# One-layer steps make their memory values behind their opening products, and sixteen output products move behind the second scores

## The chip, the cores and the metric

The kernel runs on one core of one Trainium2 chip. The metric is device time in microseconds (us) of one execution. Three runs of the kernel before gave 1603.28, 1603.80 and 1605.38; the median, 1603.8, is the time before.

## The reference

Four layers run over a sequence of 2048 tokens of width 512: a memory-augmented attention (A), a dense layer (B), and both again with the same weights, each with a layer norm ahead and a residual around it. A goes through the sequence in 64 segments of 32 tokens. Eight memory rows travel from segment to segment, so segment s cannot begin its attention before segment s-1 has given its memory:

```python
for s in range(n_seg):
    h = concat([mem, xs], axis=1)          # 8 memory rows + 32 tokens = 40
    q, k, v = h @ Wq, h @ Wk, h @ Wv       # 32 heads of 128
    scores = (q @ k.T) * scale             # masked; memory rows are seen by all
    p = softmax(where(mask, scores, -1e9))
    o = (p @ v) @ Wo                       # 40 x 512
    mem = o[:8]
    outs.append(o[8:])
```

B is `relu(h @ w1) @ w2` with 1376 hidden units.

## The kernel before

The first and the second attention layer run together, the second four segments behind the first (DELTA = 4). `step(k)` does segment k of layer 0 and segment k-4 of layer 1. So steps 4 to 63 have two layers; steps 1 to 3 have layer 0 alone, steps 64 to 67 layer 1 alone. These are the one-layer steps (`single`). Step 0 stands by itself in `first_step`.

A step runs like this on TensorE (PE):

1. `qk(0)` (L546, L532): the opening query and key products of heads 0 to 15, in three batches of 6, 6 and 4 heads, each batch first queries, then keys: six tiles `qp`. ScalarE (ACT) casts queries to `QT` (L538), VectorE (DVE) casts keys to `KT` (L540). They read `HT`, which holds 8 memory columns and 32 token columns per layer.
2. `block(k, 0, part)`: a first part of the output products of the step before (`output_x`, tile `wox`, L365, L388 or L393: attention rows of the tokens times Wo), used as filling, with pieces of value products (L306) in some steps.
3. `scores` (L566, tile `sp`), then the softmax of heads 0 to 15: maximum, subtraction, sum and reciprocal on DVE, exponential on ACT, the product `P_sb` on GpSimd (POOL).
4. `qk(1)` for heads 16 to 31, a second part of `block`, the second scores and softmax.
5. The dense layer's first product (`dense_h`, L468), the rest of `block`, the dense layer's second product (`dense_y`, L491).
6. `transpose_p` (L608), `weighted_v` (tiles `pv`, L634; reads `Vs`), `output_mem` (tile `wo`, L574: memory rows times Wo).
7. `new_memory` (L764): `wo` is cast to `wm` (L766), small products (tile `mt`, L772) turn it, and two casts copy it: to `HTm` for the values (L783) and to `HT` for queries and keys (L786). In a one-layer step the cast to `HTm` goes first; the timeline shows that the one to `HT` waits for it where the two are on different engines (step 65: "0.76 <-ACT HTm L783").
8. `memory_values(k + 1)` (L708): 32 products `vm` of 512 columns (L717) give the values of the next step's memory rows. ACT casts them (`VmS`, L721), SyncE's queue (SP) stores them to `vmd` in DRAM (L722), and `load_memory_values` (L724) reads them into `Vs` (L727) in the next step.
9. `prepare(k + 1)`: residual adds, statistics of the layer norm (L264, L219, L221), the power on POOL (L222) and the mask for the scores (L558). In a one-layer step the normalized rows `XN` (L227) are written behind the first cast of keys, by `behind` (L858, L550). `transpose_step` (L284) issues their transpose on SP (L289); `turn_p` (L614) issues that of `P_sb` (L615).

What sets the order: PE, DVE, SP and POOL run in a schedule written by hand, so their instructions stand as the program issues them, with `high_priority` only marking parts; ACT's order is chosen by the scheduler. Each engine runs its instructions in order, and a wait holds all that stands behind it on that engine.

The accumulators in PSUM that matter here are the three buffers of the pool `ps_c` (L60, tag "c"). The six tiles `qp` of `qk`, the two `vm`, `mt`, `tp`, some `pv` and, in one-layer steps, `wo` take turns in them; a tile waits until the one before it in its buffer has been read.

In step 67 (LAST) the three products of `keep_busy` (L841, tile `idle`) stand between the last part of `block` and the transposes; their result is used by nobody.

Of the kernel before, what the change touches and what calls it, by code (L numbers as in the profile page):

```python
# [22 lines left out]
def kernel(  # L23
# [260 lines left out]
    def transpose_step(k):  # L284
        if not norm_parts(k):
            return
        t = xnT_tiles[k] = wk.tile([128, NC4, 128], BF, tag="xnT", bufs=1, name="xnT")
        if k <= LAST:
            nc.sync.dma_start_transpose(out=t[:], in_=XN[:])  # L289
        else:  # L290
            tp = transpose_pe(XN)
            nc.scalar.copy(out=t[:], in_=tp[:])
# [81 lines left out]
    def output_x(k, lo, hi):  # L374
        if not 0 <= k <= LAST or ox_span(k) is None:
            return
        r0, r1 = [x % 64 for x in (ox_span(k)[0], ox_span(k)[1] - 1)]
        r1 += 1
        if lo == 0:
            pool, tag = (ps_wo, "wo") if k < LAST else (ps_c, "c")  # L380
            wo_tiles[k] = pool.tile([128, Dm], F32, tag=tag, name="wox")
        for h in range(lo, hi):
            if r1 - r0 == 64:
                halves(wo_tiles[k], OTx[:, h, r0:r1], Wo_sb[:, h, :], h == 0, h == H - 1)
            elif by_heads(k):
                for j in range(2):
                    q = 32 * (2 * (h % 2) + j)
                    nc.tensor.matmul(wo_tiles[k][q:q + 32, 0:256], lhsT=OTx[:, h, r0:r1],  # L388
                                     rhs=Wo_sb[:, h, 256 * j:256 * j + 256], start=(h < 2), stop=(h >= H - 2),
                                     tile_position=(0, q))  # L390
            else:
                for j in range(4):
                    nc.tensor.matmul(wo_tiles[k][32 * j:32 * j + 32, 0:128], lhsT=OTx[:, h, r0:r1],  # L393
                                     rhs=Wo_sb[:, h, 128 * j:128 * j + 128], start=(h == 0), stop=(h == H - 1),
                                     tile_position=(0, 32 * j))
# [290 lines left out]
    def load_values(k, act):  # L686
        for a in act:
            if a == 1 or k == 1:
                nc.sync.dma_start(out=Vs[64 * a + M:64 * a + L, :].rearrange("t (n e) -> t n e", n=NCH),
                            in_=(vd1.pop(k) if a else vd0[0])[:].rearrange("i j t e -> t (i j) e"))  # L690
            elif k >= 4 and k % 4 < 2:
                for u in range(2):
                    lo = M + 2 * M * u
                    nc.sync.dma_start(out=Vs[lo:lo + 2 * M, :].rearrange("t (n e) -> t n e", n=NCH),
                                in_=vmds[k - k % 4 - 4 + 2 * (k % 4) + u][:, :, 2 * M:32, :].rearrange("i j t e -> t (i j) e"))
            else:
                r = SEG * (k % 2)
                nc.sync.dma_start(out=Vs[M:L, :].rearrange("t (n e) -> t n e", n=NCH),
                            in_=vd0[k // 2][:, :, r:r + SEG, :].rearrange("i j t e -> t (i j) e"))
# [30 lines left out]


    def block(k, lo, hi):
        output_x(k - 1, lo, hi)
        groups = values_at(k)
        if split(k):

            rest = [(i, 0, NC4) for i in range(1, len(groups))]
            if k == 1:
                todo = [] if lo == 0 else [(0, 0, 2)] if hi == 16 else [(0, 2, NC4)] + rest
            else:  # L740
                todo = [(0, 0, 2)] if lo == 0 else [(0, 2, NC4)] if hi == 16 else rest
        else:
            todo = [(i, c4, c4 + 2) for i in range(len(groups)) for c4 in range(0, NC4, 2)
                    if lo < 8 * i + 2 * c4 + 2 <= hi]
        for i, c_lo, c_hi in todo:
            p, n = groups[i]
            values0(p, n, c_lo, c_hi, ps_wo if i in (0, 3 if len(groups) == 4 else 2) else None)
# [93 lines left out]
    def keep_busy(n):  # L841

        idle = ps_fill.tile([128, Dm], F32, tag="fill", name="idle")
        for i in range(n):
            nc.tensor.matmul(idle[:], lhsT=ident[:], rhs=Wo_sb[:, i, :], start=True, stop=True)

    def step(k):
        act = layers(k)
        single = len(act) == 1
        cont = [a for a in act if k - DELTA * a + 1 < NSEG]  # L850
        n_x = k // 4 + 3
        has_x = n_x < NXT
        by_pe = k in (1, LAST)
        ahead = has1(k + 1) or not cont
        if k % 4 == 0 and has_x:
            load_xb(n_x)
        with tc.high_priority(offset=PRIO):
            behind = norm_rows.pop(k, None)  # L858
            if k == 1:
                def behind():  # L860
                    normalize(nc.vector, xbs[n_x], xbs[n_x], moments_x(n_x), 0, 128)
            qks = qk(0, act, behind=behind)
            load_values(k, act)
            if k == 1:
                memory_values(k)
                inputs_T(n_x, True)
        part = 4 if k == LAST else 8 if single else 5
        mid = 8 if k == LAST else 16

        light = split(k)  # L870
        block(k, 0, part)
        with tc.high_priority(offset=PRIO):
            transpose_step(k)
            load_memory_values(k, act)
            scores(qks, act)
            softmax(0, act, by_pe)
            if not by_pe:
                turn_p()
        if k % 4 == 3 and has_x:
            inputs_T(n_x)  # L880
        if has0(k + 1):
            load_x(k + 1)
        if k == 1:
            load_dense()
        with tc.high_priority(offset=PRIO):
            qks = qk(1, act)
        if single:
            block(k, part, mid)
        elif light:
            dense_h(k - 2, slice(0, 1))  # L890
            block(k, part, 16)
        else:
            dense_h(k - 2)
        with tc.high_priority(offset=PRIO):
            scores(qks, act)
            softmax(1, act, by_pe)
        if single:
            dense_h(k - 2, slice(0, 1) if k == LAST else slice(None))
            block(k, mid, H)
            if k == LAST:  # L900
                keep_busy(3)
        elif light:
            dense_h(k - 2, slice(1, None))
            block(k, 16, H)
        else:
            block(k, part, H)
        f_mid = 9 if ahead or k == 2 else 5
        if k < LAST:
            dense_y(k - 2, 0, f_mid)
        if not single:  # L910
            add_output(k - 1)
        if k % 4 == 1 and k > 1 and has_x:
            mom["x"] = moments_x(n_x)
        with tc.high_priority(offset=PRIO):
            transpose_p(1)
        if ahead and k < LAST:
            dense_y(k - 2, f_mid, NFC)
        tokens_in(k + 1)
        if k < LAST and spare_T(k + 1) is not None:
            nc.gpsimd.tensor_copy(out=HTm[:, :, 2 * M:32], in_=spare_T(k + 1))  # L920
        with tc.high_priority(offset=PRIO):
            pvs = weighted_v(act)
            outputs(k, pvs)
        if single and k < LAST and ahead:
            add_dense(k - 2)
            store(k - 2)
        if single:
            add_output(k - 1, 0)
        if cont:
            with tc.high_priority(offset=PRIO):  # L930
                pool, tag = (ps_c, "c") if single else (ps_wo, "wo")
                wo = pool.tile([128, Dm], F32, tag=tag, name="wo")
                output_mem(k, wo)
        if not ahead:
            dense_y(k - 2, f_mid, NFC)
        if not single and k < LAST and ahead:
            add_dense(k - 2)
            store(k - 2)
        if cont:
            with tc.high_priority(offset=PRIO):  # L940
                new_memory(k, cont, wo)
        if single:
            add_output(k - 1, 1)
        if not ahead:
            add_dense(k - 2)
            store(k - 2)
        values1(k + 1, 1)
        if cont:
            output_ride(k)
            with tc.high_priority(offset=PRIO):  # L950
                memory_values(k + 1)
        with tc.high_priority(offset=PRIO):
            prepare(k + 1)
        if k % 4 == 2 and k > 2 and has_x:
            normalize(nc.vector, xbs[n_x], xbs[n_x], mom["x"], 0, 128)
# [83 lines left out]
```

## Time and profile before

| what | us |
|---|---|
| median of three runs | 1603.8 |
| profiled execution | 1602.88 |
| its span | 1601.2 |
| PE busy (matmul) | 1569.6 |
| PE busy (weight loads) | 1322.3 |
| DVE busy | 1263.5 |
| ACT busy | 738.6 |
| POOL busy | 347.6 |
| steps 2 and 3 | 69.3 to 108.7 |
| steps 64 to 67 with the end | 1510.9 to 1601.2 |

The granted clock of PE is 1.00 throughout. PE's matmuls overlap, so their busy time says little on how dense the work is; the starts of weight loads (PEld) show gaps better. "Idle before" at a row is the time its engine stood still ahead of it, and the name behind the arrow is what ended it; "issue" is time for which the profile shows nothing that the engine waited for.

### The profile page before, as it was taken

The page shows a single profiled execution, that of the slowest core. Times are in us where ns is not written, and L with a number is a line of the kernel's source. Part 1 is how long each engine was busy: PE and PEld are TensorE (multiplying, and loading weights), DVE is VectorE, ACT ScalarE, POOL GpSimd, SP SyncE. Part 2 cuts the span into 40 slices and gives each one's busy share as a digit, 9 for nine tenths or more (in the row PEclk, how much of TensorE's full clock was granted, in tenths as well). Part 3 has the DMA queues.
Part 4 walks back from the last instruction along what each step waited for, and adds up shares of the span by engine and source line. Part 5 has one row for each costly group of instructions (what it writes and reads, how often), then busy time and mean ns, then how long its engine had stood idle before and what let it go on. Part 6 is the DMA issues. An engine that isn't in the chain of part 4 may idle for free.

```text
span 1601.2 us, 94768 instructions
## 1 busy us (share of the span) xinstructions
PE 1569.6 (98%) x42725; PEld 1322.3 (83%) x42727; DVE 1263.5 (79%) x3112; ACT 738.6 (46%) x1800; POOL 347.6 (22%) x666
## 2 busy tenths in 40 slices
PE   6899999999999999999999999999999999999998
PEld 4677888888888888889888888888888898888876
DVE  4578888888888888888888888878888888787765
ACT  3434444444544444454444445445444544545432
POOL 2012222222222222222222222222222222221210
PEclk9999999999999999999999999999999999999999
DMA  9733343343434334334333433443343334334232
GB/s 370 234 78 74 75 89 88 66 95 86 80 75 88 86 67 97 85 78 78 87 89 63 97 86 78 79 89 87 67 101 82 80 75 82 89 62 101 69 68 39
DMA packets 222532, 146.38 MB, mean 91 GB/s; under 512 B 123976, under 2 KB 216496, under 8 KB 222128
## 3 DMA queue, kind: packets, MB, share of 16 engines
q1 hardware_dynamic: 218976, 136.09, 37.3%
q8 instruction: 335, 5.49, 1.6%
q0 software_dynamic: 3072, 4.20, 1.1%
q14 instruction: 69, 0.57, 0.1%
q10 hardware_dynamic: 80, 0.03, 0.0%
HBM read 65.41 MB, written 45.35 MB: 69 GB/s over the span
## 4 chain that ended last, share of the span: by engine, by line
PE 94%; SPq 2%; DVE 1%; issue 1%; DMA 1%; ACT 0%; POOLq 0%; ACTq 0%; DVEq 0%
PE qp L532 38%; PE wox L365 10%; PE wo L574 8%; PE vm L717 7%; PE v L346 7%; PE hp L468 6%; PE sp L491 5%; PE pv L634 4%; PE sp L566 4%; PE vp L306 3%; PE tp L608 1%; SPq L148 1%; PE xp L439 1%; SPq L134 1%; PE wox L388 1%
## 5 line engine op out<-in xcount | busy, mean ns | idle before, releaser
L538 ACT CAST QT<-qp 128x480 bf16<-128x480 f32 (+3 forms) x408 | 201.5, 494 | 392.9 <-PE qp L532 392.7
L532 PE MATMUL qp<-HT,Wq_sb 128*128 128x80 bf16 (+1 forms) x8704 | 370.2, 200 | 2.6 <-POOL HT L706 1.2
L532 PE MATMUL qp<-HT,Wk_sb 128*128 128x80 bf16 (+1 forms) x8704 | 369.3, 199 | 2.1 <-issue 1.3
L532 PEld LDWEIGHTS <-Wq_sb 128*128 128x128 bf16 x8704 | 326.4, 99 | 34.6 <-issue 27.1
L532 PEld LDWEIGHTS <-Wk_sb 128*128 128x128 bf16 x8704 | 328.5, 100 | 3.1 <-issue 2.7
L540 DVE CAST KT<-qp 128x480 bf16<-128x480 f32 (+3 forms) x408 | 225.1, 565 | 102.6 <-PE qp L532 100.5
L598 POOL TENSOR_TENSOR P_sb<-es,sm 128x320 bf16<-128x320 f32 x185 | 130.8, 721 | 752.5 <-ACT es L588 509.7
L365 PE MATMUL wox<-Wo_sb,OTx 128*64 128x256 bf16 x2880 | 173.6, 273 | 0.0
L582 DVE TENSOR_REDUCE mx<-sp 128x8 f32<-128x320 f32 x256 | 115.1, 487 | 73.5 <-PE sp L566 72.5
L593 DVE TENSOR_REDUCE sm<-es 128x8 f32<-128x320 f32 x256 | 118.9, 465 | 44.3 <-ACT es L588 33.5
L365 PEld LDWEIGHTS <-OTx 128*64 128x64 bf16 x2880 | 150.2, 110 | 2.9
L588 ACT ACTIVATE es<-es 128x320 f32<-128x320 f32 x256 | 110.5, 468 | 58.5 <-DVE es L586 57.9
L717 PE MATMUL vm<-Wv_sb,HTm 128*32 128x512 bf16 x2176 | 136.2, 380 | 0.6 <-DVE HT L786 0.6
L346 PE MATMUL v<-Wv_sb,xnT 128*32 128x512 bf16 x2048 | 129.7, 378 | 0.1
L574 PE MATMUL wo<-Wo_sb,OTm 128*32 128x512 bf16 x2144 | 129.1, 380 | 0.2
L558 DVE CAST sp<-maskb 128x320 f32<-128x320 bf16 x256 | 118.4, 484 | 0.0
L586 DVE TENSOR_TENSOR es<-sp,mx 128x320 f32<-128x320 f32 x256 | 113.8, 483 | 1.5
L717 PEld LDWEIGHTS <-HTm 128*32 128x32 bf16 x2176 | 89.3, 96 | 28.7 <-issue 11.9
L491 PE MATMUL sp<-w_sb,hT 128*64 128x256 bf16 (+4 forms) x1474 | 105.9, 276 | 0.6 <-ACT hT L474 0.5
L468 PE MATMUL hp<-xnT,w_sb 128*128 128x64 bf16 (+3 forms) x2948 | 102.5, 193 | 1.2 <-issue 0.5
L721 ACT CAST VmS<-vm 128x512 bf16<-128x512 f32 x134 | 78.6, 586 | 53.7 <-PE vm L717 53.7
L468 PEld LDWEIGHTS <-w_sb 128*128 128x128 bf16 (+1 forms) x2948 | 95.2, 101 | 2.4 <-issue 1.8
(115 smaller groups left out, 2028.8 us busy)
## 6 DMA issues: line engine op xcount, KB each, us to landing
Vs<-vd SPq DMA_DIRECT2D x96, 256.0 KB
vd<-vst SPq DMA_DIRECT2D x181, 128.0 KB
vmd<-VmS SPq DMA_DIRECT2D x134, 128.0 KB
Vs<-vmd SPq DMA_DIRECT2D x254, 32.0 KB
Vs<-vmd SPq DMA_DIRECT2D x60, 128.0 KB
Wq_sb<-in_A_Wq_dram SPq DMA_DIRECT2D x2, 2048.0 KB
Wk_sb<-in_A_Wk_dram SPq DMA_DIRECT2D x2, 2048.0 KB
Wv_sb<-in_A_Wv_dram SPq DMA_DIRECT2D x2, 2048.0 KB
```

The costliest lines, as they stand in the source:

```text
L346: nc.tensor.matmul(vp[32 * j:32 * j + 32, :], lhsT=tokens[:, c4, :], rhs=Wv_sb[:, c4, n * 512:(n + 1) * 512], start=(c4 == 0), stop=(c4 == ...
L365: nc.tensor.matmul(out[64 * j:64 * j + nr, 0:256], lhsT=lhsT, rhs=rhs[:, 256 * j:256 * j + 256], start=start, stop=stop, tile_position=(0, ...
L468: nc.tensor.matmul(hp[0:fs, fc - f0, 0:n], lhsT=w1_sb[:, c4, fc * 128:fc * 128 + fs], rhs=cols(c4), start=(c4 == 0), stop=(c4 == NC4 - 1))
L491: nc.tensor.matmul(sp_banks[bank][64 * j:64 * j + n, 0:w], lhsT=hT_tiles[d][0:fs, fc, 0:n], rhs=w2_flat[0:fs, fc * Dm + 256 * j:fc * Dm + ...
L532: nc.tensor.matmul(qp[:, hi, 0:ncol], lhsT=W_sb[:, c4, h * Dh:(h + 1) * Dh], rhs=HT[:, c4, a_lo:a_hi, :], start=(c4 == 0), stop=(c4 == NC4 ...
L538: nc.scalar.copy(out=dst[:, 0:nh, a_lo * L:a_hi * L], in_=qp[:, 0:nh, 0:ncol])
L540: nc.vector.tensor_copy(out=dst[:, 0:nh, a_lo * L:a_hi * L], in_=qp[:, 0:nh, 0:ncol])
L558: nc.vector.tensor_copy(out=sp_tiles[a], in_=maskb2)
L574: nc.tensor.matmul(wo[32 * j:32 * j + 32, :], lhsT=OTm[:, h, n, 2 * M * c:2 * M * c + 4 * M], rhs=Wo_sb[:, h, :], start=(h < 4), stop=(h > ...
L593: nc.vector.tensor_reduce(out=sm[:], in_=es[:], axis=AX.X, op=ALU.add)
L598: eng.tensor_tensor(out=P, in0=es[:], in1=sm[:].unsqueeze(2).to_broadcast([128, 8, L]), op=ALU.mult)
L717: nc.tensor.matmul(vp[32 * j:32 * j + 32, :], lhsT=HTm[:, c4, :], rhs=Wv_sb[:, c4, n * 512:(n + 1) * 512], start=(c4 == 0), stop=(c4 == NC ...
```

## The change

Three things. `memory_values(k + 1)` at the end of a step is kept only where the next step has two layers; a one-layer step makes its own memory values behind `qk(0)` and `load_values`, and there also issues its `transpose_step` (step 1 made its own already). The one-layer step's `block` is cut anew: `part` goes from 8 to 0 (from 4 to 0 in the last step), `mid` from 16 to 8 (from 8 to 4). So heads 0 to 7 go where heads 8 to 15 stood, behind `qk(1)`, and heads 8 to 15 go behind the second scores. The conditions in `block` for step 1 are rewritten so that its value products stay where they were. And `keep_busy` in the last step makes two idle products instead of three.

```diff
     def block(k, lo, hi):
+        if lo == hi:
+            return
         output_x(k - 1, lo, hi)
...
             if k == 1:
-                todo = [] if lo == 0 else [(0, 0, 2)] if hi == 16 else [(0, 2, NC4)] + rest
+                todo = [(0, 0, 2)] if lo == 0 else [(0, 2, NC4)] + rest
...
             qks = qk(0, act, behind=behind)
             load_values(k, act)
+            if single:
+                transpose_step(k)
+                memory_values(k)
             if k == 1:
-                memory_values(k)
                 inputs_T(n_x, True)
-        part = 4 if k == LAST else 8 if single else 5
-        mid = 8 if k == LAST else 16
+
+        part = 0 if single else 5
+        mid = 4 if k == LAST else 8
...
         with tc.high_priority(offset=PRIO):
-            transpose_step(k)
+            if not single:
+                transpose_step(k)
             load_memory_values(k, act)
...
             if k == LAST:
-                keep_busy(3)
+                keep_busy(2)
...
             output_ride(k)
-            with tc.high_priority(offset=PRIO):
-                memory_values(k + 1)
+            if len(layers(k + 1)) == 2:
+                with tc.high_priority(offset=PRIO):
+                    memory_values(k + 1)
```

So six steps change their order: 2, 3 and 64 to 67.

## The prediction

> **What bounds the kernel now.** I read the page first, then the waits of PE, then the timeline of the six one-layer steps that change: steps 2 and 3 (69 to 109 us) and steps 64 to 67 (1511 to 1601 us). From the page:
>
> ```profile
> PE 94%; SPq 2%; DVE 1%; issue 1%; DMA 1%; ACT 0%; POOLq 0%; ACTq 0%; DVEq 0%
> L717 PE MATMUL vm<-Wv_sb,HTm 128*32 128x512 bf16 x2176 | 136.2, 380 | 0.6 <-DVE HT L786 0.6
> q8 instruction: 335, 5.49, 1.6%
> ```
>
> The chain that ended last is PE for 94% of the span, and the change neither adds nor removes a matmul except one idle one (a pair of instructions fewer among 42,727 weight loads). So time can come only from gaps of PE in these six steps. They are small, and of two kinds.
>
> The first kind is a wait for a cast. This is the start of step 3 in the timeline (columns: start, length, engine, line, operation, count, idle time before and its releaser):
>
> ```profile
> 89.34 0.18 DVE L786 CAST HT<-mt 128x32 bf16<-128x32 f32 x1
> 89.54 1.45 PEld L717 LDWEIGHTS <-HTm 128*32 128x32 bf16 x32 [0.48 <-issue]
> 91.41 0.67 PEld L532 LDWEIGHTS <-Wq_sb 128*128 128x128 bf16 x24 [0.42 <-DVE R L371]
> ...
> 93.00 0.48 DVE L558 CAST sp<-maskb 128x320 f32<-128x320 bf16 x1
> 93.51 0.41 DVE L540 CAST KT<-qp 128x240 bf16<-128x240 f32 x1
> 93.95 1.09 DVE L227 TENSOR_SCALAR XN<-R,mv,rstd 32x512 bf16<-32x512 f32 x2
> ...
> 94.97 0.62 DVE L540 CAST KT<-qp 128x240 bf16<-128x240 f32 x2
> 95.41 0.35 PEld L566 LDWEIGHTS <-QT 128*40 128x40 bf16 x16 [0.21 <-issue]
> ```
>
> From 89.34 to 93.51 DVE is busy without a pause (residual adds, statistics, mask), and only then casts the first keys. PE hides this now: it makes the memory values (89.54 to 91.41, 1.87 us with the 0.42 in which they drain) ahead of the query and key products.
>
> The second kind is a pause that no semaphore explains ("issue"). In step 2, weight loads alone:
>
> ```profile
> 80.02 0.32 PEld L532 LDWEIGHTS <-Wk_sb 128*128 128x128 bf16 x10 [0.97 <-issue]
> 80.38 0.34 PEld L388 LDWEIGHTS <-OTx 128*32 128x32 bf16 x16
> 80.93 0.27 PEld L566 LDWEIGHTS <-QT 128*40 128x40 bf16 x16 [0.21 <-issue]
> 81.24 1.25 PEld L468 LDWEIGHTS <-w_sb 128*128 128x128 bf16 x44
> 82.52 0.78 PEld L388 LDWEIGHTS <-OTx 128*32 128x32 bf16 x32
> 83.29 0.57 PEld L491 LDWEIGHTS <-hT 128*32 128x32 bf16 x10
> 84.30 0.42 PEld L491 LDWEIGHTS <-hT 128*32 128x32 bf16 x8 [0.44 <-issue]
> ```
>
> From pause to pause are 10+16+16+44+32+10 = 128 pairs of weight load and matmul, 256 instructions. Queue q8 moved 335 packets and 5.49 MB, 16 KB each, and 85,452 PE instructions over 335 is 255. So PE's own instructions come in blocks of 256, and a block lasts at least as long as the next one takes to arrive: from pause to pause 4.28 (80.02 to 84.30), 4.27 (75.75 to 80.02), 3.75 and 3.89 (1578.26, 1582.01, 1585.90). I take 3.9, with 3.7 and 4.3 as ends. The 40-column products run at 0.025 us a pair, 3.3 us a block: too fast. [...]
>
> **The change, part by part.** The built program's order shows that it does what it says: 32 vm products go from ahead of the opening products to behind them, 16 output products (8 heads) from ahead of the first scores to behind the second, in steps 2, 3 and 64 to 67; step 1 and the two-layer steps keep their order, and so does DVE. Prices: opening products 3.3 us (step 65, 1533.46 to 1536.77); vm 1.85 (1531.61 to 1533.46); eight heads 0.55 in the old place (0.34 of loads and 0.21 of drain), 0.39 in the new one (half of the 32 at 82.52); with 64 rows (step 64) 0.8 in both.
>
> New waits. The opening products now wait for HT, cast after HTm: in steps 65 to 67 HT's cast ends 0.2 later and its signal takes 0.1, so +0.29. Then three PSUM banks serve six batches and two vm tiles, and by the built program's waits these stand behind key casts that DVE, whose order is unchanged, cannot start sooner: the first at the end of the mask, the second 1.44 us after it (1554.63 and 1556.07 in step 66; behind the two XN rows).
>
> Step 3, in full: HT ends at 89.52, products from 89.62, a batch of 24 each 0.60, so the fifth ends loading at 92.42. The sixth reuses its bank and waits for its cast: 93.05 to 93.45. vm's first tile takes the bank of the first keys: 93.92 plus 0.11 = 94.03 (in step 65 KT's cast ends at 1537.20 and the scores load at 1537.32). Its second takes that of the second keys: cast from 94.95 to 95.36, so 95.47 where the products would be there at 94.98, +0.5. Scores at 94.03 + 1.85 + 0.5 = 96.4, against 95.41: **+1.0**. Behind them the eight heads cost 0.39, of which the wait for P_sb ahead of the transposes (0.41) hides all. Counted on from 84.30, a block begins 18 pairs into vm (95.6), so the next arrives at 99.5 (needed 99.4) and the one after at 103.4 (needed 103.0): +0.5. Step 3: **+1.5**. Queued behind these waits on PE is everything up to the new memory; no other engine fills in.
>
> Step 2: DVE is free at 71.43, but the block that paused PE at 72.02 is now needed at 70.8, 54 pairs into the opening products, and I take it to come no sooner. Scores end at 76.2 (75.98 now); the pauses at 80.02 and 84.30 recur at about 80.4 (0.65) and 84.2 (0.3): **+0.15**. Step 64: start +0.3, sixth batch at 1514.07 behind the key cast, scores at 1516.4 (1517.05 now), pause 0.3 instead of 0.26, heads +0.8: **+0.15**. Step 65: +0.29, fifth batch +0.27, vm +0.6 (1536.0), scores +0.53; the pause of 0.68 at 1539.77 goes, since vm's slow instructions now stand inside that block, heads +0.39, a pause of 0.3 for one of 0.13 in the dense products: **+0.4**. Step 66: +0.29, sixth batch +0.8 (key cast 1554.63), scores +0.5; the pause of 0.41 becomes 0.55, heads +0.39: **+0.95**. Step 67: +0.28 and +0.48, scores +0.4. From here PE is paced by blocks: now 1578.26, 1582.01, 1585.90; after, the first is crossed unpaused at 1578.6, then 1582.5 and 1586.4: **+0.5**. The removed idle matmul (0.1) lies in that wait and is worth nothing.
>
> Covers. SP's queue: the transposes of XN now go ahead of the vmd stores, and turn_p behind both. In step 3 the second store issues at about 97.4, its loads some 2.5 later (I bound a landing by the 2.3 us of the R load on the page), turn_p at about 100.3, against 99.13 now; PT and Vs are needed at 105: 2 us spare. If that were gone, it would cost its excess directly on PE.
>
> Sum: 0.15 + 1.5 + 0.15 + 0.4 + 0.95 + 0.5 = **+3.65 us** on the profiled execution (span 1601.2 in a run of 1602.88, so 1.7 around it): 1606.5. The median shown, 1603.8, stands 0.9 above that run: **1607.4**.
>
> **The rivals.** A, not slower: the pauses do not come back, because vm (1.85 us for 32 pairs) now splits the run of fast products and gives the blocks time. It decides from a block arriving below 3.3 us after the last. Then step 2 gives -0.9 (the transposes follow P_sb 3.8 behind scores at 80.1), 3 +1.05, 64 -0.15, 65 +0.1, 66 +0.4, and 67 -1.3 (pv released by P_sb at about 1584.6, not by a block at 1585.90): -0.8, a median of 1603.0. For it: steps where vm, v and wo run show no pause. Against it: no interval between pauses is below 3.7. [...]
>
> B, slower still: blocks take 4.3, as in step 2, everywhere. Seven blocks of mine are limited (two in step 3, one each in 64, 65 and 66, two in 67), 0.4 each: +2.8, a median of 1610.2. For it: more DMA now meets these blocks (stores and loads beside turn_p). Against it: the last steps show 3.75 and 3.89.
>
> That the change does not happen is excluded by the built order.
>
> **How the numbers follow.** Forecast 0.6, A 0.2, B 0.2. The forecast's own spread, from blocks of 3.7 to 4.3 and cast waits 0.2 either way a step, is +2 to +5; about 0.2%, 3.2 us, is what a measurement of this kernel can tell from no change, and the forecast lies above it in 0.38 and below it in 0.22. B is all slower; A is within 0.2% but for 0.04. So slower 0.58, same 0.38, faster 0.04. The range takes in A at its lower end and B with a little: 1602.5 to 1610.8.
>
> **What would show it.** Right: in steps 3, 65 and 66 PE idle ahead of vm or of a batch of qp, released by KT (L540), and pauses by "issue" of 0.3 to 0.7 at every 128th pair; the scores of step 3 start 7.06 us after HT's cast begins, now 6.07. Wrong: no wait for KT (then the banks serve otherwise than I read), no pauses (A), or pv waiting for Vs or PT (a cover gone). If the opening cast waits fall under 0.3 a step, the change gains.

## The result, and the profile after

The changed kernel takes 1605.1 us (median of 22 runs, 1603.4 to 1609.8), the kernel before, run beside it, 1602.1 (22 runs, 1599.5 to 1605.4). The ratio is 1.0023, 95% interval 1.0016 to 1.0029: 3.7 us slower (2.6 to 4.6). The two medians alone differ by 3.0; the text goes by the ratio. The forecast was +3.65 us. Its 1607.4 stands higher mostly because it was counted from a median of three runs, 1603.8. The prediction had called 0.2% the line between slower and the same: the measured 0.23% (0.16 to 0.29) is clear of no change, but not of that line.

The page of the changed kernel, span 1603.4:

```profile
PE 89%; DVE 2%; issue 0%; ACT 0%; DMA 0%; POOLq 0%; ACTq 0%; DVEq 0%
L717 PE MATMUL vm<-Wv_sb,HTm 128*32 128x512 bf16 x2176 | 136.4, 380 | 1.3 <-DVE KT L540 1.2
q8 instruction: 335, 5.49, 1.5%
```

PE is still most of the chain that ended last (89%, before 94%). Ahead of the memory values (vm) PE now stands idle for 1.3 us instead of 0.6, and what ends it is no longer the cast of HT but the cast of keys. The instruction blocks on q8 are as many as before (335).

Step 3 in the timeline of the changed kernel:

```profile
89.05 0.18 DVE L788 CAST HT<-mt 128x32 bf16<-128x32 f32 x1
89.35 0.68 PEld L532 LDWEIGHTS <-Wq_sb 128*128 128x128 bf16 x24 [0.58 <-PE mt L774]
...
92.71 0.48 DVE L558 CAST sp<-maskb 128x320 f32<-128x320 bf16 x1
...
92.83 0.45 PEld L532 LDWEIGHTS <-Wk_sb 128*128 128x128 bf16 x15 [0.52 <-issue]
93.22 0.41 DVE L540 CAST KT<-qp 128x240 bf16<-128x240 f32 x1
...
93.69 1.05 PE L717 MATMUL vm<-Wv_sb,HTm 128*32 128x512 bf16 x16 [0.31 <-DVE KT L540]
93.69 0.74 PEld L717 LDWEIGHTS <-HTm 128*32 128x32 bf16 x16 [0.29 <-issue]
...
94.68 0.62 DVE L540 CAST KT<-qp 128x240 bf16<-128x240 f32 x2
...
95.12 1.05 PE L717 MATMUL vm<-Wv_sb,HTm 128*32 128x512 bf16 x16 [0.39 <-DVE KT L540]
95.12 0.55 PEld L717 LDWEIGHTS <-HTm 128*32 128x32 bf16 x15 [0.69 <-issue]
...
96.09 0.27 PEld L566 LDWEIGHTS <-QT 128*40 128x40 bf16 x16 [0.42 <-issue]
```

DVE is as busy as before up to its mask (92.71) and casts the first keys behind it; all 3112 of its instructions start in that trace in the order in which the program issues them. But PE has no memory values left to do in the meantime. Its sixth batch stands 0.52, the first vm tile 0.29 and the second 0.69 (weight loads), each until a buffer of `ps_c` has been read (the sixth batch until that of the fifth has, since the two others still hold keys that DVE has not cast). The scores load 7.04 us after the cast of HT begins (96.09 less 89.05); it was 6.07.

What PE waited for in the last four steps (1511 to 1602 us; total, times, longest), first the kernel before, then the changed one:

```profile
PE qp L532 <- issue: 1.4, 4, 0.6
PE pv L634 <- issue: 0.6, 1, 0.6
PE hp L468 <- issue: 0.5, 1, 0.5
```

```profile
PE qp L532 <- DVE KT L540: 1.2, 3, 0.5
PE pv L634 <- issue: 0.5, 1, 0.5
PE vm L717 <- DVE KT L540: 0.5, 1, 0.5
```

Here the wait for keys came (1.7 us; 0.3 of it, at 1583.1, stands ahead of the second key products of step 67 and is no part of the opening), and most of the pauses by issue went (2.5 to 0.5). That is why the two executions differ by little in these steps. The lengths of the steps, from the weight load of one step's mt to that of the next, in us:

| kernel | 2 | 3 | 4 to 63 | 64 | 65 | 66 | 67 and end | span |
|---|---|---|---|---|---|---|---|---|
| before | 20.19 | 18.83 | 1402.2 | 20.72 | 19.67 | 19.39 | 31.46 | 1601.2 |
| changed | 19.52 | 19.97 | 1403.8 | 20.75 | 19.54 | 19.88 | 30.88 | 1603.4 |
| e1_first | 20.26 | 19.97 | 1403.5 | 20.44 | 19.08 | 18.75 | 30.84 | 1601.8 |
| e2_last | 18.74 | 18.83 | 1402.7 | 20.65 | 19.55 | 19.71 | 31.49 | 1600.4 |
| e3_mem_only | 18.90 | 20.16 | 1405.0 | 20.66 | 19.85 | 19.72 | 30.72 | 1603.9 |
| e4_heads_only | 19.34 | 19.07 | 1404.5 | 20.89 | 19.09 | 19.64 | 31.28 | 1602.5 |
| e5_act_keys | 19.09 | 18.97 | 1402.4 | 20.49 | 18.85 | 19.44 | 29.58 | 1597.7 |
| e6_before_act_keys | 19.51 | 18.60 | 1403.2 | 20.58 | 19.13 | 19.34 | 30.05 | 1599.6 |
| e7_shift | 19.21 | 20.40 | 1410.1 | 20.65 | 19.63 | 19.70 | 31.07 | 1611.0 |
| e8_before_shift | 19.06 | 18.82 | 1409.3 | 20.39 | 19.79 | 18.78 | 30.98 | 1607.2 |
| e9_q_first | 19.41 | 18.70 | 1404.1 | 20.64 | 18.75 | 19.18 | 30.02 | 1600.5 |
| e10_turn_first | 19.90 | 18.69 | 1402.3 | 20.86 | 18.75 | 18.90 | 30.09 | 1598.5 |
| e11_shift_128 | 19.28 | 19.96 | 1404.1 | 21.44 | 19.55 | 20.16 | 30.84 | 1607.7 |
| e12_shift_32 | 18.08 | 19.96 | 1406.5 | 20.66 | 19.55 | 19.70 | 33.03 | 1606.5 |

Each row is one execution. Step 3 repeats to 0.02 us between kernels with the same order in it, unless a pause falls into it; step 2 and the last one do not, since pauses by issue come and go there.

### The profile page after: what moved, and what is told of

It reads as the page before. It is cut to its first block, busy times and chain, and to the rows that moved or that the text cites. A ratio compares the mean times of both kernels' runs of the same rounds, so it can differ in the third digit from the quotient of the medians.

```text
span 1603.4 us, 94769 instructions
## 1 busy us (share of the span) xinstructions
PE 1569.7 (98%) x42724; PEld 1323.5 (83%) x42726; DVE 1262.6 (79%) x3112; ACT 738.0 (46%) x1800; POOL 346.7 (22%) x666
## 4 chain that ended last, share of the span: by engine, by line
PE 89%; DVE 2%; issue 0%; ACT 0%; DMA 0%; POOLq 0%; ACTq 0%; DVEq 0%
PE qp L532 35%; PE wox L365 10%; PE wo L574 7%; PE vm L717 7%; PE v L346 7%; PE hp L468 5%; PE sp L491 5%; PE pv L634 4%; PE sp L566 4%; PE vp L306 3%; PE tp L608 1%; PE xp L439 1%; PE wox L388 0%; PE mt L774 0%; DVE sm L593 0%
```

## The experiments

Each ratio is against runs of the kernel before on the same chip. A reading in microseconds is the ratio less 1, times 1602.

**Which part, and which steps.** The four kernels differ from the changed one by two lists, the steps whose memory values are moved (OWN) and those whose output products are (LATE); step 1 is always in both:

```diff
-            if single:
+            if k in OWN:
                 transpose_step(k)
                 memory_values(k)
...
-        part = 0 if single else 5
-        mid = 4 if k == LAST else 8
+        part = 0 if k in LATE else 4 if k == LAST else 8 if single else 5
+        mid = (4 if k == LAST else 8) if k in LATE else 8 if k == LAST else 16
...
-            if len(layers(k + 1)) == 2:
+            if k + 1 not in OWN:
```

e1_first makes the whole change in steps 2 and 3 alone:

> The change in steps 2 and 3 alone; steps 64 to 67 as before. My theory (the price is the waits for the key casts and the moved instruction pauses, where the prediction put them): slower than before by 1.65 us (0.15 in step 2, 1.5 in step 3). Rival 1 (in the six steps the change costs only what the two profiled executions show, the rest of the measured 3.7 us is not in them): step 2 gains 0.7, step 3 loses 1.1, so +0.5. Rival 2 (the loss is in the last steps): 0.

Measured: 1602.8 us, ratio 1.0008 (0.9999 to 1.0017), +1.3 us.

e2_last makes it in steps 64 to 67 alone:

> The change in steps 64 to 67 alone. My theory: +2.0 us (0.15, 0.4, 0.95, 0.5). Rival 1 (as the two profiled executions show: 0.0, -0.1, +0.5, and the last step with the end -0.6): -0.2. If this and the run with steps 2 and 3 alone add up to much less than 3.7 us, something outside the six steps takes part.

Measured: 1603.2 us, ratio 1.0012 (1.0003 to 1.0021), +1.9 us. The two halves add up to 3.2, near the whole. The interval of the first reaches just below nothing, but its step 3 takes 19.97, as in the changed kernel, against 18.83: the price comes from both ends.

e3_mem_only moves the memory values in all six steps and leaves the output products in their old place:

> The memory values move behind the opening products in steps 2, 3 and 64 to 67, but the output products of heads 0 to 15 stay where they were. My theory (moving the memory values is what meets the key casts, the heads only change which cover they give): +2.5 to +3.7 us, with PE waiting for KT ahead of vm as in the changed kernel. Rival (the heads taken from ahead of the first scores are the loss): 0, or a gain.

Measured: 1605.6 us, ratio 1.0028 (1.0017 to 1.0039), +4.5 us (2.7 to 6.2), above the range that I gave.

e4_heads_only moves the output products and leaves the memory values:

> The output products move as in the change, but the memory values stay at the end of the step before. My theory: the first scores have no cover left and wait for the last key cast, so they start no sooner, and the heads cost their 0.39 (0.8 in step 64) later, less 0.41 of wait for P_sb in step 3: +1 to +2 us. Rival (the heads are the whole loss): +3 to +3.7. Rival (fewer instructions ahead of the second products give the instruction blocks time): 0 or a gain.

Measured: 1601.8 us, ratio 1.0003 (0.9993 to 1.0013), +0.5 us (-1.1 to 2.1). My theory for it missed: its first scores do start sooner, by 0.55 us in step 3, and wait for a key cast (0.30) only after the first six. The page has the same verdict in the idle time of vm. The line of e3_mem_only is word for word that of the changed kernel above (1.3, of it 1.2 for KT); that of e4_heads_only:

```profile
L717 PE MATMUL vm<-Wv_sb,HTm 128*32 128x512 bf16 x2176 | 136.2, 380 | 0.6 <-DVE HT L788 0.6
```

So the move of the memory values is the price; that of the sixteen output products costs and brings nothing that these runs can tell from zero.

**Is it the wait for keys?** It could still be the later place of the scores by itself. The wait can be taken away without touching the order on PE, SP or POOL: ACT makes the opening key casts of the six steps, each right behind the query cast of its batch.

```diff
-            qks = qk(0, act, behind=behind)
+            qks = qk(0, act, behind=behind, keys=nc.scalar.copy if k in (2, 3, 64, 65, 66, 67) else nc.vector.tensor_copy)
...
-                nc.vector.tensor_copy(out=dst[:, 0:nh, a_lo * L:a_hi * L], in_=qp[:, 0:nh, 0:ncol])
+                keys(out=dst[:, 0:nh, a_lo * L:a_hi * L], in_=qp[:, 0:nh, 0:ncol])
```

In the changed kernel:

> The changed kernel, but in the six one-layer steps the three key casts of the opening products are made by ACT instead of DVE, each behind the query cast of its batch. Nothing on PE, SP or POOL changes its order. Theory (the waits for key casts that stand behind DVE's statistics are the price of the change): step 3, 19.97 us in the changed kernel, falls by 1.0 to 1.4, step 66 by 0.5 to 0.8, steps 65 and 67 by 0.2 to 0.4 each; the whole comes down from 3.7 us over the kernel before to 0.5 to 1.7 over it (ratio 1.0003 to 1.0010). Rival (the price is the place of the memory values itself, that scores and softmax start later and the pauses of PE fall elsewhere, while the cast waits are hidden): step 3 stays at 19.7 or more and the ratio at 1.0020 to 1.0025.

Measured: 1600.6 us, ratio 0.9989 (0.9980 to 0.9997): 1.8 us faster than the kernel before, and some 5.5 under the changed one, more than I had expected (0.5 to 1.7 over the kernel before). In the profiled executions the six steps together fell by 4.1, and the untouched steps 4 to 63 by 1.5. Steps 3 and 65 fell by 1.00 and 0.69, step 66 by 0.44 (with a pause of 0.59 in it), step 67 with the end by 1.30. The rows of step 3:

```profile
91.36 0.36 ACT L540 CAST KT<-qp 128x240 bf16<-128x240 f32 x1 [0.19 <-PE qp L532]
```

```profile
92.05 1.42 PEld L717 LDWEIGHTS <-HTm 128*32 128x32 bf16 x32
93.89 0.27 PEld L566 LDWEIGHTS <-QT 128*40 128x40 bf16 x16 [0.42 <-issue]
...
103.44 0.88 PEld L634 LDWEIGHTS <-Vs 40*128 40x128 bf16 x32 [0.80 <-issue]
```

The second keys are cast at 91.36 instead of 94.68 at the earliest, all 32 vm products load in one piece, and on the page the idle time of vm is 0.0. The scores load 5.45 us after the cast of HT begins (88.44). That is 1.59 sooner than in the changed kernel. But the gap ahead of pv grows from 0.21 to 0.80, which the view of waits puts down to PT, so 1.00 is left of it in step 3.

In the kernel before, the same edit:

> The kernel before with the same edit: the opening key casts of the six one-layer steps on ACT. Theory: here the memory values stand ahead of the opening products and hide DVE's statistics, so the casts are not waited for and the time stays within 0.1% (ratio 0.9992 to 1.0008), step 3 at 18.6 to 18.9 us. Rival (faster key casts free something else, so that the previous kernel of this batch gains by the edit and not by the waits): it gains as much as the changed kernel does, 2 us or more (ratio 0.9988 or less).

Measured: 1601.5 us, ratio 0.9996 (0.9987 to 1.0004); step 3 is 18.60. Faster key casts alone do nothing that can be measured where nobody waits for them (by the interval at most 2.1 us, against the 5.5 above). So the gain of the version above is the wait, and the wait is the price of the change.

**What is left of the opening.** HT ahead of HTm at the end of steps 1, 2 and 64 to 66, with ACT's key casts:

```diff
-        for f in (to_values, to_queries) if single else (to_queries, to_values):
+        for f in (to_values, to_queries) if single and k not in (1, 2, 64, 65, 66) else (to_queries, to_values):
```

> The changed kernel with ACT's opening key casts, and with HT cast ahead of HTm at the end of steps 1, 2 and 64 to 66, as the products need them now. Theory (what is left of the opening waits is the order of these two casts): the opening products of steps 2 and 3 start 0.1 us and those of steps 65 to 67 0.2 to 0.3 us sooner behind the mt products, together 0.5 to 1.0 us under the version with the key casts alone; ratio to the kernel before 0.9980 to 0.9988. Rival (the pauses of PE and the waits behind give it back): the casts come sooner and the ratio stays at 0.9989, the gain reappearing ahead of tp or pv.

Measured: 1601.7 us, ratio 1.0001 (0.9992 to 1.0010), which misses the range that I gave. In the trace the edit does what it should: the wait ahead of step 3's opening products falls from 0.58 to 0.42, steps 3, 65 and 66 by 0.27, 0.10 and 0.26. But steps 2 and 64, the opening and the untouched steps 4 to 63 came out longer by 0.3, 0.2, 0.7 and 1.8 in this execution, and the median shows no gain. Pauses come and go by more than the edit is worth.

e10_turn_first goes after the 0.7 to 0.8 us ahead of pv, by moving the transpose of P_sb ahead of the loads of Vs on SP's queue in steps 2 and 3:

```diff
-            load_memory_values(k, act)
+            if k not in (2, 3):
+                load_memory_values(k, act)
             scores(qks, act)
             softmax(0, act, by_pe)
             if not by_pe:
                 turn_p()
+            if k in (2, 3):
+                load_memory_values(k, act)
```

> The version with HT first, and in steps 2 and 3 the DMA transpose of P_sb (turn_p) ahead of the loads of the memory values on SP's queue. With ACT's key casts pv of step 3 waited 0.80 us for PT, since turn_p stood behind those loads and was issued at 99.06 where P_sb was there at 97.5. Theory: turn_p is issued at about 97.6, PT lands before pv, and step 3 falls by 0.5 to 0.8 to about 18.2 to 18.4 us. Rival (Vs, whose loads now go last, takes PT's place as the late one): pv of step 3 waits for Vs, 0.4 us or more, and step 3 stays at 18.8 or more.

Measured: 1601.7 us, ratio 0.9999 (0.9991 to 1.0008), step 3 at 18.69 against 18.70. What PE waited for in step 3, first with HT first, then with turn_p moved as well:

```profile
PE pv L634 <- DMA PT<-P_sb: 0.5, 1, 0.5
```

```profile
PE pv L634 <- DMA Vs<-vmd: 0.3, 1, 0.3
```

The rival held, a little smaller than I gave it: Vs takes PT's place. The memory values go through DRAM and back on the queue that also transposes P_sb, and one of the two is last.

These three versions with ACT's key casts stand at 0.9989, 1.0001 and 0.9999. The first alone beats both kernels in its interval; together they say that without the wait the change is worth between nothing and 2 us.

**The instruction blocks.** The forecast counts pauses from a block of 256 PE instructions. If that is right, idle matmuls early in the program move every later boundary:

```diff
+        fill = ps_fill.tile([128, Dm], F32, tag="fill", name="early")
+        for i in range(64):
+            nc.tensor.matmul(fill[:, 0:8], lhsT=ident[:], rhs=ident[:, 0:8], start=True, stop=True)
         masks(0)
```

Half a block (64 pairs) in the changed kernel:

> The changed kernel with 64 idle matmuls of 8 columns (128 instructions of PE, half a block) ahead of the first masks, in the opening in which PE waits for weights; nothing else. Theory (a block of 256 PE instructions is what pauses PE): every pause by issue in steps 2, 3 and 64 to 67 moves by 64 pairs of weight load and matmul, the same instructions that paused before run through, and new ones pause 64 pairs from them; the steps' lengths change by the pauses, 0.2 to 1.0 us each, in both directions, the whole by under 2 us either way. Rival (the pauses belong to certain instructions, a switch of shape or a full buffer): the pauses stay at the same instructions (80.0 in front of the 11th key product of the second batch, 125.3 and 128.9).

Half a block in the kernel before:

> The kernel before with the same 64 idle matmuls ahead of the first masks. Theory as for the changed kernel: the pauses of steps 2, 65, 66 and 67 move by 64 pairs; the sum of them, 5.5 us in the profiled execution, may come to 3 to 7, and the time within 0.15% of the kernel before. Rival: pauses stay where they are.

A whole block (128 pairs) in the changed kernel:

> The changed kernel with 128 idle matmuls of 8 columns ahead of the first masks: a whole block of 256 instructions, where 64 of them cost 9.4 us against the kernel before and 64 were half a block. Theory (the place of the block boundaries in the two-layer steps costs the 6.3 us by which steps 4 to 63 grew, 1403.8 to 1410.1): a whole block puts every boundary back at the same instruction, steps 4 to 63 take 1402 to 1405 again, and only the opening is longer, by 1.2 us or up to twice that; ratio to the kernel before 1.003 to 1.004. Rival (the idle matmuls or what they delay cost the time, whatever the boundaries): steps 4 to 63 stay at 1409 or more.

A quarter (32 pairs) in the changed kernel:

> The changed kernel with 32 idle matmuls of 8 columns, a quarter of a block. Theory of the block boundaries: pauses move by 32 pairs; steps 4 to 63 come out between 1401 and 1411, by where the boundaries fall in the query and key products, and not as half of what 64 added; the opening grows by 0.6. Rival (the idle matmuls cost the time): steps 4 to 63 grow by half of 6.3, to about 1407.

Measured: e7_shift 1611.9 us, ratio 1.0050 (1.0036 to 1.0065); e8_before_shift 1607.6, 1.0033 (1.0021 to 1.0046); e11_shift_128 1610.2, 1.0054 (1.0042 to 1.0067); e12_shift_32 1606.6, 1.0031 (1.0019 to 1.0042).

The pauses move as they should. The opening products of step 2 are 128 pairs. Their loads around the pause in the changed kernel, with half a block more, and with a whole block more:

```profile
71.03 0.22 PEld L532 LDWEIGHTS <-Wq_sb 128*128 128x128 bf16 x6
71.73 0.52 PEld L532 LDWEIGHTS <-Wq_sb 128*128 128x128 bf16 x18 [0.48 <-issue]
```

```profile
73.72 0.22 PEld L532 LDWEIGHTS <-Wk_sb 128*128 128x128 bf16 x6
75.00 0.32 PEld L532 LDWEIGHTS <-Wk_sb 128*128 128x128 bf16 x10 [1.06 <-issue]
```

```profile
74.39 0.22 PEld L532 LDWEIGHTS <-Wq_sb 128*128 128x128 bf16 x6
75.58 0.52 PEld L532 LDWEIGHTS <-Wq_sb 128*128 128x128 bf16 x18 [0.97 <-issue]
```

It stands behind 54 pairs (24+24+6), then behind 118 (24+24+24+24+16+6), 64 later, then behind 54 again. With a quarter, step 2 shows no such pause at all and is the shortest of the table (18.08): a boundary does not always cost something. In step 3, by contrast, the gap of 0.69 stays in front of the same vm product at half a block (95.90 in that trace): a wait for a cast, not a pause. These readings, one staying and the other moving, separate the two kinds of gap.

My bound on the whole, under 2 us, was wrong, in both kernels. In the profiled executions half a block made steps 4 to 63, of which nothing else was changed, longer by 6.3 (changed kernel) and 7.0 (before); with a whole block they took 1404.1, against 1403.8 without a shift. The opening pays for the matmuls themselves, 1.1 us for 64 in the changed kernel (1.4 in the kernel before) and 3.4 for 128 (more than I had expected). So in these executions it is not the number of idle matmuls that costs the sixty steps their time, but by how much of a block they shift the program. How it does is open: in the changed kernel the gaps at the boundaries themselves come to 3.8 us in steps 4 to 63 with half a block more, against 2.7 without, and most of the rest stands in the six steps shown in the last section.

The runs as a whole say it more weakly. Both executions with half a block that were profiled are the slowest of their five (1608.0 to 1612.8 and 1604.1 to 1609.0). By the ratios, half a block costs the changed kernel 4.3 us (8.0 less 3.7) and the kernel before 5.3; less the opening, 3 to 4 us are left for the sixty steps. A whole block costs 5.0 (8.7 less 3.7), of which 1.6 is left. With intervals of some 2 us each way, the runs alone do not separate 3.2 from 1.6. The quarter gave 1406.5 in its profiled execution, the slowest of seven, near the 1407 of its rival; it cannot tell the two apart.

## Why the prediction was right, and where it was not

**The wait for keys, right.** From the mt load of the step before to the first scores, before and changed, with the forecast of the difference: step 3, 6.52 and 7.50 (+0.98; forecast +1.0); step 64, 7.11 and 6.59 (-0.52; -0.65); step 65, 6.66 and 7.01 (+0.35; +0.53); step 66, 6.66 and 7.17 (+0.51; +0.5); step 67, 6.44 and 6.92 (+0.48; +0.4). In steps 3 and 65 to 67 the mechanism is the one worked out: three buffers, eight tiles, and a cast of keys behind DVE's statistics. In step 64 it is not: the forecast had the sixth batch wait for a cast there, and in the changed kernel PE waits for nothing that the view of waits shows; the scores come sooner because sixteen output products no longer stand ahead of them. e5_act_keys took the cast away and with it the loss.

**The output products, right.** In e4_heads_only the first scores of step 3 come 0.55 sooner (5.97 behind the mt load, against 6.52) and the second at the same 10.82, and behind these 48 of the products stand where 32 stood (in the changed kernel 1.21 us, against 0.78). As forecast, the one about pays for the other: that kernel is within 0.2% of the kernel before.

**The pauses, wrong in their places and in part in their sign.** The forecast carried the boundaries on from step to step as if one execution held for all: +0.5 in step 3, pauses of 0.3 and 0.55 in steps 65 and 66, +0.5 in step 67. In the changed kernel step 3 has no pause; its 1.14 us (18.83 to 19.97) are the wait and little else, against 1.5 forecast. Step 65 came out at 19.54 or 19.55 in four executions with the whole change (before, 19.08 to 19.79), step 66 has one pause of 0.18, step 67 one of 0.64 within pv. The step that failed is "Counted on from 84.30, a block begins 18 pairs into vm (95.6), so the next arrives at 99.5". The grid of 128 pairs is real, as the shifts showed (54, 118 and 54 pairs), but what a boundary costs changes from one execution to the next: behind the same 54 pairs of step 2 it was 0.48 us in the changed kernel and 0.97 with a whole block more. In the last four steps of the profiled pair the pauses even shrank (2.5 to 0.5 us), as rival A had it, for which the vm products between the opening products and the scores give the blocks time; that this is the reason was not tried by itself. A was wrong about the size: the 0.9 and 1.3 us that it took off steps 2 and 67 are not there on the average (step 67 with the end took 31.46 and 30.84 with the old order, 30.88 and 31.49 with the new).

**The sum.** Right at +3.65 against +3.7, in part by errors that cancel. Averaged over the executions above without the shifts, kernels with the change in the steps in question against those without, step 3 is +1.14 and steps 64 to 67 +1.05 (90.18 for before and e1_first, 91.23 for changed and e2_last; but before and e1_first, with the same order, differ by 2.1 there, so that the +1.05 is weak); step 2 cannot be told within its scatter of 0.8 either way. That is 2.2 of the 3.7. The rest, if it is more than scatter (the interval begins at 2.6), would lie in step 2 or in the untouched steps 4 to 63, which took 1402.2 to 1405.0 in all executions without a shift by part of a block. The place of the boundaries is no difference there: counted in the traces (weight load, matmul and semaphore instructions of PE), 4323 instructions stand ahead of the mt load of step 3 and 82,064 ahead of that of step 64, the same in both kernels. Whether they are longer in the changed kernel on the average stays open: one profile of each kernel cannot tell it, and no kernel here was profiled often enough.

**The cover on SP's queue.** The 2 us of spare time that I gave turn_p held in the changed kernel (no wait for PT ahead of pv in step 3). In e5_act_keys it was used up, with scores 1.6 us sooner: there the gap ahead of pv grew by 0.59.

## What to carry to other kernels

Work that is moved behind the products it used to precede can take its cover with it (here the first scores of step 3 came 0.98 us later): ask which engine had been catching up behind it (here DVE's statistics ahead of the key casts), and whether the buffers let PE go on without that engine. Before giving up such a move, look for an idle engine that can take the late cast (with the casts on ACT, step 3 fell from 19.97 to 18.97 us). And a difference of 0.2% between two kernels with different instruction counts may come from the place of their instruction blocks: half a block of shift made steps 4 to 63 longer by 6.3 and 7.0 us in the profiled executions, 0.4% of the whole. Count the instructions ahead of the stretch in question in both: here they were the same. Where they differ, a version with half a block of idle pairs and one with a whole block help to tell, with enough runs of each.

## What the hardware showed that I had not expected

Half a block of shift cost about as much as the change itself: 6.3 and 7.0 us over sixty steps in the profiled executions, 3 to 4 by all runs. A pause there can cost twice. In the changed kernel with half a block more, step 10:

```profile
260.27 1.02 PE L532 MATMUL qp<-HT,Wk_sb 128*128 128x80 bf16 x24 [0.61 <-issue]
260.35 0.49 DVE L582 TENSOR_REDUCE mx<-sp 128x8 f32<-128x320 f32 x1 [1.32 <-PE qp L532]
...
263.19 1.17 DVE L540 CAST KT<-qp 128x480 bf16<-128x480 f32 x2
...
263.85 0.74 PE L532 MATMUL qp<-HT,Wk_sb 128*128 128x80 bf16 x16 [0.26 <-DVE KT L540]
```

PE pauses 24 pairs behind the scores; DVE's second maximum starts only when PE goes on; the softmax holds up the cast of keys, and the last batch waits for it. Without the shift neither gap is there, and this step takes 23.39 us instead of 24.58. Six steps of that trace (10, 46, 50, 54, 55 and 58) show this pair of gaps in the weight loads, the first of 0.36 to 0.81 us at the 247th to 265th pair of the step, the second of 0.18 to 0.43, together 5.8. By my count of instructions these pauses stand 13 to 58 instructions short of a boundary, where those of steps 2 to 4 and 36 stand on it within 2. Why is open, and with it whether these are the same kind of pause; that a whole block removes the time rests on one execution. The second gap also comes without the first: in the changed kernel without a shift it stands in steps 26 and 27 (0.34 and 0.43), where in step 27 DVE's sum had waited 1.21 for ACT's exponential.

The runs agree with the blocks of 256 instructions that the forecast counted (54, 118 and 54 pairs), and the traces of the two kernels tie the pauses to the packets of q8, of 16 KB each: the pauses of step 2 in the kernel before (72.02, 75.75, 80.02 and 84.30) end 1.34 to 1.51 us after a packet has ended, those in the changed kernel (71.73, 80.01 and 84.02) 1.45 to 1.50. By count most crossings show no gap: of some 330 in the changed kernel's trace, 13 have one over 0.15 us in front of the weight load at the boundary, some of them gaps that stand at a change of shape anyway. But in the rows of step 2 above, where products of 40 columns follow each other, a crossing left gaps of 0.48, 0.97 and 1.06 us, the longest about a third of the 3.7 us that the whole change costs.
